# Where a fused kernel adds its weight sums: GpSimd, VectorE, and the buffers around them

## The chip, the cores and the metric

One core of one Trainium2 chip runs the whole program. The metric is the device time of one execution in microseconds (us), as a median of several executions. TensorE is the matrix engine, VectorE, ScalarE and GpSimd are the three elementwise engines; in the profile they are PE, DVE, ACT and POOL, and PEld is TensorE's loading of weights. PSUM is the memory into which TensorE writes; a bank is one of the kernel's tiles there, of 128 x 512 fp32, and its pools hold eight at a time (4 and 4 in the first chunk, then 3 for attention, 2 A, 1 B and 2 o). SBUF is the memory of the other tiles.

## The reference, cut to what matters

```python
B, H, S, D = 4, 8, 768, 48            # attention: a gated linear recurrence, fp32
f = 1 / (1 + exp(-f_logit))
for t in range(S):
    state = f[:, :, t, :, None] * state + einsum('bhd,bhe->bhde', k[:, :, t], v[:, :, t])
    y[:, :, t] = einsum('bhd,bhde->bhe', q[:, :, t], state)
x = y.transpose(0, 2, 1, 3).reshape(3072, 384)
out = (silu(x @ w_gate) * (x @ w_val)) @ w_out      # 384 -> 1536 -> 384, fp32
```

## The kernel before

The kernel works in six chunks of 128 positions for each of the four batches, so 512 tokens a chunk. While the feed-forward part of chunk c is written, attention of chunk c+1 is woven between its steps. A scheduler that knows the dependences orders each engine's instructions at build time; what the program writes first is not always what runs first.

The first chunk uses plain products. While they run, the weights still arrive and are joined from pieces by VectorE (four operations a piece: L455, L457, L458, L459). From the second chunk on, the two up projections are made by a scheme with 15 products of thirds instead of 18, and the down projection by one with 7 products of halves instead of 8. These need sums of weight blocks: 16 adds for the even 128-blocks, 16 for the odd ones, 4 for the down weights.

```python
# (cut) one group of 15 products, a "triple": (PSUM bank, weight block, token block)
PRODUCTS = [("A", "a11", "t14"), ("B", "a23", "t8"), ("o", "a21", "b22"),
            ("A", "a12", "t2"), ("B", "e3", "b32"), ("o", "e0", "t1"),
            ("A", "e5", "t9"), ("B", "e2", "t5"), ("c", "a13", "b11"),
            ("A", "e4", "t4"), ("B", "a33", "t15"), ("c", "a31", "t10"),
            ("A", "a32", "t11"), ("B", "e1", "t3"), ("A", "a22", "b21")]
...
def aside(name):                       # ScalarE copies the bank to SBUF, and so frees it
    return copy(name, "aside", bufs=3)
def finish(i, n, src):
    nc.scalar.activation(dst, src[:, 0, :], AF.Silu)              # L858 before, L848 after
    nc.vector.tensor_tensor(dst, dst, src[:, 1, :], ALU.mult)
...
                    elif r == 12:
                        minus(got[31], got[31], aside("A"))
                        finish(2, 0, got[31])
                    elif r == 13:
                        plus(got[11], got[11], p["B"])            # VectorE reads bank B itself
                        finish(0, 0, got[11])
                    else:
                        finish(1, 0, p["A"])
...
for c in range(NCH):
    if c == 0:
        hidden, last = mlp_plain(c)
        ...                                                       # the joins are put between steps
        pieces = hidden + [lambda: weight_sums(0, nc.gpsimd)] + last
    else:
        hidden, last = mlp_fifteen(c)
        pieces = hidden + last
    take_turns(pieces, attention_steps(c + 1) if c + 1 < NCH else [], 2 if c else 8)
    if c == 0:
        early.close()                                             # the first chunk's pools end here
        comb = ctx.enter_context(tc.tile_pool(name="comb", bufs=1))
        banks.append(ctx.enter_context(tc.tile_pool(name="bps", bufs=3, space=bass.MemoryType.PSUM)))
        banks_a, banks_b, banks_o = (
            ctx.enter_context(tc.tile_pool(name=f"{n}ps", bufs=k, space=bass.MemoryType.PSUM))
            for n, k in (("A", 2), ("B", 1), ("o", 2)))
        make_rooms(comb)
        load(SQUARES * B)
        down_weight_sums()
        weight_sums(1, nc.vector)
```

Lines to know: L666 are the first chunk's up projections, L690 its output products, L695 the copies of its outputs. L844 is the product of a triple (L834 after the change), L849 ScalarE's copy (L839), L933 and L987 the down products (L923 and L977). L728 and L731 are VectorE's add and subtract, wherever they are called from.

## Time and profile before

| | before |
|---|---|
| time, median of three runs | 674.54 us (673.98 to 674.97) |
| profiled span | 670.9 us |
| TensorE, VectorE, ScalarE, GpSimd busy | 628.1, 507.5, 273.9, 48.3 us |

The profiled execution took 672.67 us.

The lines that carry the argument are shown in the prediction. How the span divides: Four marks on TensorE cut it: the first up projection (L666), the first product of a triple (L844), and of the last down product (L987), which every chunk from the second on has, its first group in the program and its last but one.

| stretch of the kernel before | from, to (us) | long |
|---|---|---|
| opening | 0, 37.90 | 37.90 |
| first chunk | 37.90, 169.39 | 131.49 |
| second chunk | 169.39, 271.91 | 102.52 |
| third to sixth chunk | 271.91, 660.36 | 388.45 |
| closing | 660.36, 670.9 | 10.5 |

The opening is the same code in every kernel here, and it takes 36.3 to 38.1 us whatever the kernel; so below the first chunk is measured from its own start.

### The profile page before, as it was taken

The numbers are of one execution on the slowest core, as the hardware profiler recorded it, in microseconds if no ns is written. First come the engines' busy times: TensorE is split into PE (matmuls) and PEld (weight loads), VectorE is DVE, ScalarE is ACT, GpSimd is POOL, SyncE is SP. The second block draws the span as 40 slices with busy tenths as digits, with TensorE's granted clock in tenths as the row PEclk, the third lists the DMA queues.
The fourth block names the chain that finished last, engine by engine and source line by source line (L and its number), as shares of the span: only waits on it lengthen the run. The fifth ranks groups of instructions, "written<-read, shape, count | busy, mean of one in ns | idle before, by whom it ended". The sixth has DMA issues, their size and how long they took to land.

```text
span 670.9 us, 10581 instructions
## 1 busy us (share of the span) xinstructions
PE 628.1 (94%) x3894; PEld 503.5 (75%) x3894; DVE 507.5 (76%) x905; ACT 273.9 (41%) x504; POOL 48.3 (7%) x58
## 2 busy tenths in 40 slices
PE   7999999399999799999899999899999899999996
PEld 4955554165788689887689987679987689988895
DVE  5889689989789697579797679778769974457741
ACT  1466454110675352373471164461165440156500
POOL 1000008700000020000010000000000000000000
PEclk9999999599999799999999999999999989999999
DMA  9997543103323223402223401313302200100001
GB/s 176 212 222 215 139 152 110 59 4 110 111 56 81 55 60 88 113 25 74 69 59 86 117 24 48 95 48 91 104 19 57 65 22 13 60 2 1 0 1 52
DMA packets 98397, 51.92 MB, mean 77 GB/s; under 512 B 56864, under 2 KB 92192, under 8 KB 98336
## 3 DMA queue, kind: packets, MB, share of 16 engines
q1 hardware_dynamic: 95024, 46.63, 29.3%
q10 hardware_dynamic: 3312, 4.52, 1.9%
q8 instruction: 33, 0.54, 0.3%
q14 instruction: 28, 0.23, 0.1%
HBM read 42.47 MB, written 4.72 MB: 70 GB/s over the span
## 4 chain that ended last, share of the span: by engine, by line
PE 50%; DVE 20%; issue 5%; SPq 4%; ACT 4%; DMA 3%; POOL 0%; ACTq 0%; DVEq 0%; POOLq 0%
PE o L933 13%; PE A L844 11%; PE B L844 9%; PE o L844 4%; SPq L593 3%; DVE c L731 3%; PE c L844 3%; PE o L690 2%; PE sc L552 2%; PE o L987 2%; PE y L582 1%; DVE qT L532 1%; DMA xT<-yT 1%; DVE c L728 1%; DVE A L554 1%
## 5 line engine op out<-in xcount | busy, mean ns | idle before, releaser
L844 PE MATMUL A<-xs,w_both 128*128 128x256 f32 x240 | 65.5, 395 | 3.7 <-ACT ob L695 2.1
L933 PE MATMUL o<-w_out,h 128*128 128x192 f32 x360 | 62.5, 330 | 0.0
L933 PEld LDWEIGHTS o<-w_out,h 128*128 128x128 f32 x360 | 58.2, 190 | 1.8 <-ACT c L950 0.6
L844 PE MATMUL B<-xs,w_both 128*128 128x256 f32 x160 | 43.9, 397 | 14.4 <-DVE c L728 14.4
L858 ACT ACTIVATE h<-c 128x256 f32<-128x256 f32 x100 | 40.5, 416 | 40.1 <-DVE c L731 38.0
L844 PEld LDWEIGHTS A<-xs,w_both 128*128 128x128 f32 x240 | 46.1, 197 | 11.8 <-ACT ob L695 2.7
L849 ACT COPY c<-A 128x512 f32<-128x512 f32 x40 | 23.3, 583 | 74.8 <-PE A L844 41.0
L544 POOL TENSOR_TENSOR decayed<-state,tails 128x192 f32<-128x192 f32 x20 | 19.0, 950 | 476.8 <-DVE state L610 349.3
L849 ACT COPY aside<-A 128x512 f32<-128x512 f32 x60 | 35.1, 586 | 44.4 <-PE A L844 44.4
L728 DVE TENSOR_TENSOR c<-c,aside 128x512 f32<-128x512 f32 x40 | 28.1, 702 | 31.5 <-ACT aside L849 31.5
L731 DVE TENSOR_TENSOR c<-c,aside 128x512 f32<-128x512 f32 x60 | 41.7, 695 | 7.3 <-ACT aside L849 7.0
L690 PE MATMUL o<-w_out,h 128*128 128x384 f32 x96 | 35.0, 519 | 13.0 <-DVE h L682 13.0
L859 DVE TENSOR_TENSOR h<-h,c 128x256 f32<-128x256 f32 x100 | 41.1, 422 | 6.5 <-ACT h L858 6.5
L844 PEld LDWEIGHTS B<-xs,w_both 128*128 128x128 f32 x160 | 29.3, 193 | 20.9 <-DVE c L728 16.6
L844 PE MATMUL B<-xT,extra 128*128 128x256 f32 x160 | 42.3, 388 | 0.0
L731 DVE TENSOR_TENSOR c<-o,c 128x512 f32<-128x512 f32 x40 | 27.8, 694 | 18.8 <-PE o L844 17.4
L844 PE MATMUL c<-xT,w_both 128*128 128x256 f32 x160 | 41.2, 380 | 0.0
L844 PE MATMUL A<-xs,extra 128*128 128x256 f32 x160 | 41.2, 380 | 0.0
L933 PE MATMUL o<-ws,h 128*128 128x192 f32 x240 | 40.9, 326 | 0.0
L933 PEld LDWEIGHTS o<-ws,h 128*128 128x128 f32 x240 | 39.1, 190 | 0.1
L690 PEld LDWEIGHTS o<-w_out,h 128*128 128x128 f32 x96 | 18.7, 201 | 27.2 <-DVE h L682 14.8
L519 DVE TENSOR_TENSOR_SCAN tails<-gates,ones 128x516 f32<-128x516 f32 x24 | 30.5, 1270 | 8.9 <-POOL decayed L544 6.7
(140 smaller groups left out, 1245.8 us busy)
## 6 DMA issues: line engine op xcount, KB each, us to landing
fsquares<-in_f_logit_dram SPq DMA_DIRECT2D x64, 96.0 KB, 2.3
ksquares<-in_k_dram SPq DMA_DIRECT2D x64, 96.0 KB, 2.3
qsquares<-in_q_dram SPq DMA_DIRECT2D x64, 96.0 KB, 2.3
v<-in_v_dram SPq DMA_DIRECT2D x24, 192.0 KB, 3.6
w<-in_moe_w_gate_dram SPq DMA_DIRECT2D x6, 768.0 KB, 4.6
w<-in_moe_w_val_dram SPq DMA_DIRECT2D x6, 768.0 KB, 5.0
w<-in_moe_w_out_dram SPq DMA_DIRECT2D x6, 768.0 KB, 4.5
out_dram<-ob ACTq DMA_DIRECT2D x23, 192.0 KB, 2.1
```

The source lines that it names most:

```text
L519: nc.vector.tensor_tensor_scan(tail[:, 0:n][:, ::-1], gate[:, 0:n][:, ::-1], ones[:, ::-1], 1.0, op0=ALU.mult, op1=ALU.add)
L544: nc.gpsimd.tensor_tensor(decayed[:, :, 0:D], states[b], whole.broadcast_to((128, HP, D)), ALU.mult)
L552: nc.tensor.matmul(sc[par][:, a * C:(a + 1) * C], lhsT=kT[r, a, :], rhs=qT[r, a, :], start=True, stop=True)
L593: nc.sync.dma_start(out=xT[c][f % 128:f % 128 + n, f // 128, b * C:(b + 1) * C], in_=yT[r:r + n, par, a // 2 * C:(a // 2 + 1) * C])
L690: nc.tensor.matmul(p, lhsT=h[n // 2][:, n % 2 * 2 + b // 2, b % 2 * C:(b % 2 + 1) * C], rhs=w_out[:, j, :], start=(n == 0), stop=(n == NF ...
L728: (engine or nc.vector).tensor_tensor(dst, a, b, ALU.add)
L731: (engine or nc.vector).tensor_tensor(dst, a, b, ALU.subtract)
L844: nc.tensor.matmul(p[name][:, n, :], lhsT=weights_of[a][:, n, cols], rhs=tokens[b], start=fresh and n == 0, stop=True, skip_group_check=True)
L849: nc.scalar.copy(t, p[name])
L858: nc.scalar.activation(dst, src[:, 0, :], AF.Silu)
L859: nc.vector.tensor_tensor(dst, dst, src[:, 1, :], ALU.mult)
L933: nc.tensor.matmul(p[:, n, :], lhsT=lhsTs[j][:, n * C:(n + 1) * C], rhs=rhs[:, j, :], start=first and j == 0 and n == 0, stop=j == NP - 1, ...
```

## The change

The intent: GpSimd's sums slow VectorE (a 128x512 sum took 1.75 us beside them and 0.68 without), so VectorE makes them all, placed where they are needed and no sooner; bank B, the only single one, is freed by ScalarE and not by the busy VectorE; and the banks A, B and o are laid where they come free earlier.

```diff
-            pieces = hidden + [lambda: weight_sums(0, nc.gpsimd)] + last
+            pieces = hidden + weave(last, weight_sums(0))           # in pairs, by VectorE
         else:
             hidden, last = mlp_fifteen(c)
+            if c == 1:
+                half = len(hidden) // 2
+                hidden = hidden[:1] + weave(hidden[1:half], weight_sums(1)) + hidden[half:]
+                hidden.append(lambda: behind(down_weight_sums))
...
-            banks.append(ctx.enter_context(tc.tile_pool(name="bps", bufs=3, ...)))
-            banks_a, banks_b, banks_o = (... for n, k in (("A", 2), ("B", 1), ("o", 2)))
+            banks_a, banks_b, banks_o, later = (... for n, k in (("A", 2), ("B", 1), ("o", 2), ("b", 3)))
+            banks.append(later)
             make_rooms(comb)
             load(SQUARES * B)
-            down_weight_sums()
-            weight_sums(1, nc.vector)
...
-                        plus(got[11], got[11], p["B"])
+                        plus(got[11], got[11], aside("B"))
...
+    def behind(f):                     # edges: what f writes on VectorE runs after what was written before
+        n = len(traced)
+        last = next(ins for ins in reversed(traced) if ins.engine == mybir.EngineType.DVE)
+        f()
+        keep_order([last] + [ins for ins in traced[n:] if ins.engine == mybir.EngineType.DVE])
```

More of the change, by code (lines that the diff above doesn't have):

```diff
@@ L725, in short_path, with plus, minus @@
     sums = {}
-    def plus(dst, a, b, engine=None):
-        (engine or nc.vector).tensor_tensor(dst, a, b, ALU.add)
-    def minus(dst, a, b, engine=None):
-        (engine or nc.vector).tensor_tensor(dst, a, b, ALU.subtract)
+    def plus(dst, a, b):
+        nc.vector.tensor_tensor(dst, a, b, ALU.add)
+    def minus(dst, a, b):
+        nc.vector.tensor_tensor(dst, a, b, ALU.subtract)
     def minus_both(dst, a, b):
@@ L745, in weight_parts, with weight_sums @@
         return w, e
-    def weight_sums(odd, engine):
+    def weight_sums(odd):
         w, e = weight_parts()
@@ L751, in weight_sums @@
         a11, a12, a13, a21, a22, a23, a31, a32, a33 = (w[i, k] for i in range(3) for k in range(3))
-        add, sub = (lambda d, x, y: plus(d, x, y, engine)), (lambda d, x, y: minus(d, x, y, engine))
-        sub(e[0], a11, a12)
-        add(e[1], a12, a33)
-        add(e[1], e[1], a13)
-        sub(e[2], e[1], a11)
-        sub(e[3], e[0], a13)
-        add(e[4], a21, a32)
-        sub(e[5], a12, a21)
-        sub(a11, a12, a23)
-        add(a13, e[3], a21)
-        add(e[3], e[3], a23)
-        add(a13, a13, a31)
-        sub(a13, a13, a33)
-        sub(a21, a22, a21)
-        add(a22, a22, a23)
-        add(a22, a22, a32)
-        sub(a31, a32, a31)
+        return [lambda f=f, d=d, x=x, y=y: f(d, x, y) for f, d, x, y in (
+            (minus, e[0], a11, a12), (plus, e[1], a12, a33), (plus, e[1], e[1], a13), (minus, e[2], e[1], a11),
+            (minus, e[3], e[0], a13), (plus, e[4], a21, a32), (minus, e[5], a12, a21),
+            (minus, a11, a12, a23), (plus, a13, e[3], a21), (plus, e[3], e[3], a23), (plus, a13, a13, a31),
+            (minus, a13, a13, a33), (minus, a21, a22, a21), (plus, a22, a22, a23), (plus, a22, a22, a32),
+            (minus, a31, a32, a31))]
     down_sums = {}
@@ L993, in down_seven, with weave @@
         return hidden_sums, [one, two, three, four]
+    def weave(first, second):
+        second = [second[i:i + 2] for i in range(0, len(second), 2)]
+        woven = []
+        for i, f in enumerate(first):
+            woven += [f] + [lambda fs=fs: behind(lambda: [g() for g in fs]) for fs in
+                            second[i * len(second) // len(first):(i + 1) * len(second) // len(first)]]
+        return woven
+    def behind(f):
[3 more added lines that the diff above has]
+        keep_order([last] + [ins for ins in traced[n:] if ins.engine == mybir.EngineType.DVE])
     def take_turns(first, second, rest):
@@ L1073, in short_path @@
             comb = ctx.enter_context(tc.tile_pool(name="comb", bufs=1))
-            banks.append(ctx.enter_context(tc.tile_pool(name="bps", bufs=3, space=bass.MemoryType.PSUM)))
-            banks_a, banks_b, banks_o = (
+            banks_a, banks_b, banks_o, later = (
                 ctx.enter_context(tc.tile_pool(name=f"{n}ps", bufs=k, space=bass.MemoryType.PSUM))
-                for n, k in (("A", 2), ("B", 1), ("o", 2)))
+                for n, k in (("A", 2), ("B", 1), ("o", 2), ("b", 3)))
+            banks.append(later)
             make_rooms(comb)
             load(SQUARES * B)
-            down_weight_sums()
-            weight_sums(1, nc.vector)
         if c == NCH - 2:
```

## The prediction

> **What bounds the kernel now.** I read the page's busy shares first, then its forty slices, then the lists of waits, then TensorE and VectorE in order of time around the slices where TensorE is not full.
>
> ```profile
> PE 628.1 (94%) x3894; PEld 503.5 (75%) x3894; DVE 507.5 (76%) x905; ACT 273.9 (41%) x504; POOL 48.3 (7%) x58
> PE   7999999399999799999899999899999899999996
> POOL 1000008700000020000010000000000000000000
> PEclk9999999599999799999999999999999989999999
> ```
>
> TensorE is the bound nearly everywhere. Its hole, in slice eight (117 to 134 us), lies where GpSimd is busy, and the granted clock drops there too. TensorE's own timeline, start and duration first, the wait in brackets:
>
> ```profile
> 114.52 1.56 PE L690 MATMUL o<-w_out,h 128*128 128x384 f32 x4
> 123.40 1.65 PE L690 MATMUL o<-w_out,h 128*128 128x384 f32 x2 [7.33 <-DVE h L682]
> 130.76 5.16 PE L690 MATMUL o<-w_out,h 128*128 128x384 f32 x10 [5.71 <-DVE h L682]
> 149.00 18.33 PE L690 MATMUL o<-w_out,h 128*128 128x384 f32 x56
> 169.39 1.13 PE L844 MATMUL A<-xs,w_both 128*128 128x256 f32 x4 [2.06 <-ACT ob L695]
> 223.56 2.07 PE L844 MATMUL B<-xs,w_both 128*128 128x256 f32 x4 [3.80 <-DVE c L728]
> 330.32 1.13 PE L844 MATMUL B<-xs,w_both 128*128 128x256 f32 x4 [3.03 <-DVE c L728]
> ```
>
> The first chunk's output products (L690) stop 7.3 and 5.7 us: two of their four PSUM banks hold the last two up projections until VectorE has multiplied them into h. The next chunk's first product then waits 2.06 us for the last output copy. Later stops are on bank B, whose last sum VectorE reads. Why is h late? VectorE in order of time, the same operations with GpSimd running (first three) and after it (last three):
>
> ```profile
> 116.00 1.61 DVE L457 TENSOR_SCALAR top<-top 128x768 int32<-128x768 int32 x1
> 117.54 1.75 DVE L731 TENSOR_TENSOR extra<-extra,w_both 128x512 f32<-128x512 f32 x1
> 119.21 2.01 DVE L458 SCALAR_TENSOR_TENSOR top<-w,top 128x768 int32<-128x768 int32 x1
> 133.58 0.80 DVE L457 TENSOR_SCALAR top<-top 128x768 int32<-128x768 int32 x1
> 134.31 0.68 DVE L728 TENSOR_TENSOR extra<-w_both 128x512 f32<-128x512 f32 x1
> 134.91 0.94 DVE L458 SCALAR_TENSOR_TENSOR top<-w,top 128x768 int32<-128x768 int32 x1
> ```
>
> Each SBUF operation costs about one microsecond more while GpSimd's sixteen sums run (102.4 to 129.0 us). VectorE also does odd-block weight sums ahead of the h products: the scheduler had hoisted work written later. The waits' totals (sum, count, longest):
>
> ```profile
> PE B L844 <- DVE c L728: 14.4, 7, 3.8
> ACT h L858 <- DVE c L731: 38.0, 33, 3.2
> ```
>
> The first line: seven stops of TensorE on bank B. The second: ScalarE too is held by VectorE.
>
> [...] Here the 3.80 us stop was followed by products of about 1.7 us instead of 0.86, the 3.03 us stop by none.
>
> **The change part by part.**
>
> *GpSimd's sums go.* From 102.7 to 130.1 us VectorE ran, at slow durations, three L457 (4.86 us), two L455 (3.25), two L458 (4.03), two L459 (3.47), five adds (8.78) and a scan (2.28). At undisturbed durations (0.56, 0.56, 0.96, 0.95, 0.68, 1.22) they take 1.68, 1.12, 1.92, 1.90, 3.40 and 1.22. The excess is 26.67 - 11.24 = 15.4 us. The five odd-block adds (3.4 us undisturbed) are also put behind later work. So the two h products, done at 123.3 and 130.7, should follow their matmuls, the last of which ends near 112.5.
>
> *What TensorE then needs.* Unstopped from 112.44: 96 output matmuls at 0.327 (18.33/56) are 31.4 us; attention between them (2.1 + 0.9 + 1.6 + 2.6) 7.2. That ends at 151.0, and the next chunk's first product now starts at 169.4: at most 18.4 us, of which 13.0 are the stops, 2.9 slow clock behind them (1.65 - 0.65 and 5.16 - 3.27), 2.06 plus a few tenths the boundary. The PSUM rearrangement is aimed at the last: A, B and o come onto banks that attention held, and not the output products.
>
> *VectorE in that stretch.* Four joins of 3.03 us (12.1), attention 6.3, two h 1.4, sixteen even-block sums at 0.68 now moved here (10.9), eleven token sums (4.1): 34.8 of 38.6 us. It fits, tightly. With the weave, by the step arithmetic, the last attention step comes after output step six and not after step four, so five steps (13.1 us) follow it and not seven. Its copy, transfer and token sums took 148.3 to 161.0, or 12.7 us. So the first product will be at 151 to 157; I choose 154.4, a gain of 15.
>
> *The second chunk pays.* It ran from 169.4 to 273.9. Up to 243.8 VectorE was busy 12.75 + 14.28 + 14.95 + 17.04 = 59 of 74.4 us (windows). The odd-block sums add 16 x 0.68 = 10.9 to its first half; about 8 us of the next attention, done at 161 to 170 ahead of the boundary, move behind it. That is 78 us of VectorE against 67 of TensorE (74.4 less the 3.80 stop and 3.2 of slow clock): VectorE becomes its bound, say 81 with little idle time. The four down-weight sums (1.34 to 1.36 each, 5.4 us) go to the output stage, where VectorE is busy 24.2 of 30.2: perhaps 1 us. That is +7 us from this view. Counting only VectorE's whole work from 112 to 274 (137.6 less about 10 of contention plus 12 net sums, 140, against 162 elapsed) with 8 us idle leaves the two chunks together 14 shorter, not 8. I take 11.
>
> *Bank B.* Twenty copies on ScalarE (0.586 each, 11.7 us in all, at 41% busy) replace a wait for VectorE; the adds stay at 0.68 to 0.70. The stops in chunks three to five are 1.01 + 3.03 + 0.67 + 3.04 + 0.42 + 2.48 = 10.7 us. ScalarE sits behind VectorE itself in its SiLU, and the next triple's third A product needs a ScalarE copy in that same queue, so a stop of 3 us can give about two products, 1.7 us: 5.1 + 1 of the small ones, 6 us of 10.7.
>
> Sum: -11 - 6 = -17 us gives 657.5; I put 1.5 us of it aside for order effects of a static schedule: 659.0 us.
>
> **The rivals.** *VectorE takes over entirely.* For it: the 78 against 67 us[...]. Against: today's own stop at 223.6 came from such a burst and cost only 7. It would eat the gain: 666 to 672. *The stops go whole.* For it: the h products have nothing left to wait for, chunk two's half-clock stretch may vanish, ScalarE has room for B. Then 18 + 10, less 3: near 649. *The boundary is hidden by transfers:* if the last attention step, written later, makes the xT transfers (issue to 154.98, landing at 156.4) end no sooner relative to the output products, the token sums set the start and the gain falls to 10: about 664.
>
> **Range and chances.** The sizes that I am least sure of are the second chunk (+0 to +12) and B (0 to -11); the 15 us rest on stops seen in the trace. So 648 to 668 for 8 in 10. Two per cent of 674.54 is 13.5, so "faster" means under 661.0: my value lies 2 us on that side, chance 0.57; within 2% 0.41; slower 0.02.
>
> **What would show it.** GpSimd busy near 19 + 3 us without sums; no VectorE L457 or L458 over 1.2 us; the L690 stops gone and the clock full in slice eight; the first "A" product at 151 to 157 without a wait on the output copy; sixteen 128x512 adds among the second chunk's first two triples, VectorE over 90% busy there, and new TensorE stops; that chunk longer than 104.5 us; the waits of B on L728 gone, A or B waiting on ScalarE instead. I am wrong if the two long stops stay in another form (a join, a transfer), or if the second chunk loses over 12 us.

## The result, and the profile after

| | before | after |
|---|---|---|
| time, median of four runs each | 674.75 us (673.98 to 676.73) | 643.21 us (642.67 to 644.62) |
| ratio | | 0.9531 (0.9506 to 0.9557) |
| profiled span | 670.9 us | 641.5 us |
| first chunk | 131.49 | 112.52 |
| second chunk | 102.52 | 100.46 |
| third to sixth chunk | 388.45 | 381.96 |
| opening and closing | 48.4 | 46.6 |

A ratio here and below is the mean time of one kernel's fast runs over the mean of the other's fast runs of the same rounds, so it is not quite the ratio of the medians that stand beside it. The kernel after ran in two more batches, at 0.9576 and 0.9583; the mean of its three ratios, 0.956, is what its variants are held against.

The gain is twice the predicted one: 31.5 us by the medians, against 15.5. The time lies below the range of 648 to 668. By the two profiles the gain is 29.4 us, because the profiled execution of the kernel before was a short one.

The page of the kernel after, first the busy times, then the forty slices of TensorE, GpSimd and TensorE's granted clock:

```profile
PE 615.1 (96%) x3894; PEld 495.8 (77%) x3894; DVE 498.4 (78%) x921; ACT 286.6 (45%) x526; POOL 29.9 (5%) x42
PE   7999999999998999999899999899999999999996
POOL 1000000000000050000020000020000000000000
PEclk8999999999999999999999999999999999999999
```

The hole in TensorE's eighth slice is gone, and so are all slices with a lowered clock after the first; before there were three of them. TensorE's busy time itself fell by 13 us with the same 3894 matmuls: a busy time is shorter at full clock (four products of bank B behind a stop took 1.13 us at full clock, at 306.43 in the kernel after, and 2.07 at half clock, at 223.56 in the kernel before). Windows of the three stretches split each into TensorE's busy time and the rest of its length, its idle time:

| stretch | before: busy + idle | after: busy + idle | less busy | less idle |
|---|---|---|---|---|
| first chunk | 116.24 + 15.25 | 112.52 + 0.00 | 3.72 | 15.25 |
| second chunk | 98.12 + 4.40 | 94.69 + 5.77 | 3.43 | -1.37 |
| third to sixth | 375.24 + 13.21 | 371.53 + 10.43 | 3.71 | 2.78 |

Of the 27.5 us that the three stretches lost, 16.7 are stops and 10.9 are shorter busy time. Most of the latter is slow clock: in these stretches TensorE was busy for 18.0 us at half clock in the kernel before and not at all in the kernel after, and half of that is 9.0. In what follows, "lost at half clock" is this half, an estimate from the trace.

TensorE in order of time at the end of the first chunk:

```profile
110.72 2.75 PE L690 MATMUL o<-w_out,h 128*128 128x384 f32 x8
113.74 5.33 PE L690 MATMUL o<-w_out,h 128*128 128x384 f32 x16
...
136.21 13.17 PE L690 MATMUL o<-w_out,h 128*128 128x384 f32 x40
149.22 1.03 PE L834 MATMUL A<-xs,w_both 128*128 128x256 f32 x4
```

No bracket, so no wait: the output products run through, and the first product of a triple follows them without a stop. The VectorE lines of that stretch answer to those of the prediction; the last of these four is its longest idle time there:

```profile
110.39 0.56 DVE L457 TENSOR_SCALAR top<-top 128x768 int32<-128x768 int32 x1
110.87 0.68 DVE L682 TENSOR_TENSOR h<-h,val 128x512 f32<-128x512 f32 x1
111.47 0.95 DVE L458 SCALAR_TENSOR_TENSOR top<-w,top 128x768 int32<-128x768 int32 x1
...
136.40 0.35 DVE L610 TENSOR_TENSOR state<-decayed,dS 128x192 f32<-128x192 f32 x1 [2.93 <-PE dS L606]
```

The join operations are back at 0.56 and 0.95 us, where they had taken 1.61 and 2.01 beside GpSimd, and the last product of h is written at 111.5 and not at 130.7 us. VectorE even waits for TensorE.

Windows give the busy time of each engine in a stretch. The second chunk up to its down products, of the kernel before:

```profile
core 0: us, PE busy (x) PEld busy (x) DVE busy (x) ACT busy (x) POOL busy (x), PEclk, DMA share, GB/s
169.39:243.80 74.41, 70.01 (x445) 57.06 (x445) 59.02 (x106) 44.85 (x84) 1.34 (x2) 0.95 0.28 74
```

The end of the first chunk and the same part of the second, of the kernel after:

```profile
110.72:149.22 38.50, 38.50 (x227) 24.27 (x226) 29.63 (x53) 9.04 (x15) 1.07 (x4) 1.00 0.20 51
149.22:220.78 71.56, 66.51 (x445) 54.53 (x444) 70.46 (x127) 46.83 (x87) 1.86 (x3) 1.00 0.34 88
```

VectorE is busy 70.46 of 71.56 us, 98%. Yet this part is shorter than it was before, when VectorE was busy 59.02 of 74.41. TensorE's stops in it, beside waits of under half a microsecond, are two:

```profile
179.11 1.16 PE L552 MATMUL sc<-qT,kT 48*128 48x128 f32 x16 [1.38 <-DVE qT L540]
199.90 1.16 PE L552 MATMUL sc<-qT,kT 48*128 48x128 f32 x16 [1.97 <-DVE qT L540]
```

In the third to sixth chunk bank B no longer waits for VectorE, but it still waits, for ScalarE's copy (TensorE's timeline of the kernel after):

```profile
306.43 1.13 PE L834 MATMUL B<-xs,w_both 128*128 128x256 f32 x4 [2.46 <-ACT aside L839]
...
407.85 1.13 PE L834 MATMUL B<-xs,w_both 128*128 128x256 f32 x4 [1.62 <-ACT aside L839]
```

ScalarE's own order of time shows why: its copy of B stands behind a SiLU that waits for VectorE.

```profile
305.48 0.42 ACT L848 ACTIVATE h<-c 128x256 f32<-128x256 f32 x1 [3.57 <-DVE c L731]
305.81 0.57 ACT L839 COPY aside<-B 128x512 f32<-128x512 f32 x1
```

### The profile page after: what moved, and what is told of

It is laid out like the page before. It is cut to its first block, busy times and chain, and to the rows that moved or that the text cites.

```text
span 641.5 us, 10613 instructions
## 1 busy us (share of the span) xinstructions
PE 615.1 (96%) x3894; PEld 495.8 (77%) x3894; DVE 498.4 (78%) x921; ACT 286.6 (45%) x526; POOL 29.9 (5%) x42
## 4 chain that ended last, share of the span: by engine, by line
PE 60%; DVE 19%; SPq 7%; DMA 5%; ACT 3%; issue 3%; POOL 0%; DVEq 0%; ACTq 0%; POOLq 0%
PE o L923 13%; PE A L834 9%; PE B L834 8%; SPq L593 5%; PE gate L666 5%; PE val L666 5%; PE sc L552 3%; PE o L834 3%; PE o L690 3%; DVE c L731 3%; PE c L834 2%; PE o L977 2%; PE y L582 2%; DMA ksquares<-in_k_dram 2%; DVE tails L519 1%
## 5 line engine op out<-in xcount | busy, mean ns | idle before, releaser
L834 PE MATMUL A<-xs,w_both 128*128 128x256 f32 x240 | 63.1, 383 | 3.6 <-ACT c L839 2.4
L728 DVE TENSOR_TENSOR c<-c,aside 128x512 f32<-128x512 f32 x60 | 41.9, 698 | 26.8 <-ACT aside L839 26.7
L923 PEld LDWEIGHTS o<-w_out,h 128*128 128x128 f32 x360 | 58.1, 190 | 2.8 <-DVE w_out L731 0.6
L848 ACT ACTIVATE h<-c 128x256 f32<-128x256 f32 x100 | 40.4, 416 | 34.8 <-DVE c L731 30.9
L834 PEld LDWEIGHTS A<-xs,w_both 128*128 128x128 f32 x240 | 44.2, 190 | 11.6 <-ACT c L839 4.1
L544 POOL TENSOR_TENSOR decayed<-state,tails 128x192 f32<-128x192 f32 x20 | 27.0, 1351 | 480.4 <-DVE state L610 331.7
L834 PE MATMUL B<-xs,w_both 128*128 128x256 f32 x160 | 42.6, 388 | 6.2 <-ACT aside L839 5.7
L731 DVE TENSOR_TENSOR c<-c,aside 128x512 f32<-128x512 f32 x60 | 41.7, 696 | 5.8 <-ACT aside L839 5.6
L839 ACT COPY aside<-B 128x512 f32<-128x512 f32 x60 | 35.0, 583 | 13.1 <-PE B L834 13.1
L731 DVE TENSOR_TENSOR c<-o,c 128x512 f32<-128x512 f32 x40 | 27.8, 696 | 10.6 <-PE o L834 8.8
L552 PEld LDWEIGHTS sc<-qT,kT 48*128 48x128 f32 x384 | 25.0, 187 | 14.0 <-issue 10.0
```

What stands on the lines that cost most here:

```text
L544: nc.gpsimd.tensor_tensor(decayed[:, :, 0:D], states[b], whole.broadcast_to((128, HP, D)), ALU.mult)
L552: nc.tensor.matmul(sc[par][:, a * C:(a + 1) * C], lhsT=kT[r, a, :], rhs=qT[r, a, :], start=True, stop=True)
L728: nc.vector.tensor_tensor(dst, a, b, ALU.add)
L731: nc.vector.tensor_tensor(dst, a, b, ALU.subtract)
L834: nc.tensor.matmul(p[name][:, n, :], lhsT=weights_of[a][:, n, cols], rhs=tokens[b], start=fresh and n == 0, stop=True, skip_group_check=True)
L839: nc.scalar.copy(t, p[name])
```

## The experiments

The theory is the prediction's: GpSimd's contention with VectorE made the first chunk's hole, bank B made the later stops, and each part of the change acts where it seems to. The rivals: the gain comes from moving and holding the sums, whoever makes them; or from the PSUM pools, which the prediction gave two microseconds; or the second chunk is better for a reason of its own. The experiments ran in four batches on three chips (the first and the last batch on the same one), each beside the kernel before (medians 673.21, 673.40, 673.17 and 672.37).

The marks, in us, from the profiled execution of each kernel:

| kernel | median | ratio to before | first chunk | second | third to sixth |
|---|---|---|---|---|---|
| before | 674.75 | 1 | 131.49 | 102.52 | 388.45 |
| after | 643.21 | 0.9531 | 112.52 | 100.46 | 381.96 |
| e6_after_again | 646.13 | 0.9576 | 112.51 | 101.65 | 383.12 |
| e14_after_third | 645.42 | 0.9583 | 112.51 | 102.15 | 381.28 |
| e1_gpsimd_back | 654.86 | 0.9720 | 123.25 | 101.89 | 381.48 |
| e2_vector_only | 663.50 | 0.9859 | 120.54 | 102.24 | 388.24 |
| e3_pools_back | 649.22 | 0.9640 | 115.73 | 102.58 | 382.06 |
| e4_b_back | 653.89 | 0.9708 | 112.51 | 100.17 | 393.04 |
| e5_no_edges | 643.37 | 0.9548 | 114.42 | 98.21 | 382.29 |
| e7_fewer_odd (wrong numbers) | 642.29 | 0.9527 | 112.51 | 98.34 | 383.18 |
| e8_half_early | 643.42 | 0.9548 | 112.51 | 99.48 | 382.87 |
| e9_copy_first | 646.92 | 0.9605 | 112.51 | 101.02 | 384.35 |
| e10_both | 646.89 | 0.9604 | 112.51 | 100.88 | 384.42 |
| e11_b_only | 661.69 | 0.9820 | 132.11 | 100.23 | 380.86 |
| e12_pools_only | 664.87 | 0.9878 | 129.67 | 95.95 | 389.35 |
| e13_three_parts | 645.08 | 0.9588 | 119.40 | 98.03 | 380.65 |

### e1: the even sums back on GpSimd

```diff
-            pieces = hidden + weave(last, weight_sums(0))
+            pieces = hidden + [lambda: [f() for f in weight_sums(0, nc.gpsimd)]] + last
```

(The functions of the sums take an engine again.)

> The changed kernel with one part undone: the sixteen even-block sums run on GpSimd again, after the last up projection, as before; the odd-block sums stay in the second chunk. Contention theory[...]: joins and adds between 100 and 130 us last 1.6 to 2.0 us again, about 10 to 15 us of excess, the first product of the second chunk starts at 155 to 163 us instead of 149.2, the whole takes 650 to 657 us. Order theory (the gain came from holding the odd-block sums back): h is multiplied in time all the same, first product by 152, whole within 3 us of 643.2.

Measured: 654.86 us, 0.972 (0.9689 to 0.975) of before, so 1.6% of 673, 11 us, over the kernel after. The first chunk is 10.7 us longer and nothing else is. TensorE's timeline has the stop again, and VectorE's has the slow joins, one fence for each:

```profile
120.98 1.65 PE L690 MATMUL o<-w_out,h 128*128 128x384 f32 x2 [6.06 <-DVE h L682]
```

```profile
114.84 1.61 DVE L457 TENSOR_SCALAR top<-top 128x768 int32<-128x768 int32 x1
118.31 2.02 DVE L458 SCALAR_TENSOR_TENSOR top<-w,top 128x768 int32<-128x768 int32 x1
```

The durations are those of the kernel before to within 0.01 us, with everything else of the change in place. The edit also takes the weaving of these sums away; e2 changes their engine alone. Together they show that the engine of these sums is what stretches VectorE's work and stops TensorE.

### e2: the even sums by VectorE, and nothing else

```diff
-            pieces = hidden + [lambda: weight_sums(0, nc.gpsimd)] + last
+            pieces = hidden + [lambda: weight_sums(0, nc.vector)] + last
```

> The kernel before with one part done: the sixteen even-block sums on VectorE, nothing held, nothing else changed. Contention theory: no instruction of VectorE over 1.4 us there, the first product at 151 to 158 instead of 169.4, whole 656 to 663 us. Order theory: some 28 sums of 0.6 us (17 us) stand ahead of the last two h products, so TensorE's stops on L690 stay at 8 us or more, first product after 162, whole 667 to 673 us.

Measured: 663.50 us, 0.9859 (0.9829 to 0.9889): 9.5 us of gain, all in the first chunk (10.95 us shorter). It does not reach the kernel after's first chunk, because a shorter stop stands in place of the two:

```profile
120.52 7.12 PE L690 MATMUL o<-w_out,h 128*128 128x384 f32 x16 [3.41 <-DVE w_out L459]
...
157.30 1.13 PE L844 MATMUL A<-xs,w_both 128*128 128x256 f32 x4 [2.09 <-ACT ob L695]
```

TensorE now waits for a join and not for h: the sixteen even sums stand on VectorE between 101.6 and 116.6 us, ahead of that join's operations. The time is half a microsecond above the expected 656 to 663. The 16 products after the stop take 7.12 us where they take 5.33 at full clock. The 2.09 us at the boundary stay, and the second chunk's 3.80 us stop on B stays too.

### e3: the old PSUM pools in the new kernel

```diff
-            banks_a, banks_b, banks_o, later = (... for n, k in (("A", 2), ("B", 1), ("o", 2), ("b", 3)))
-            banks.append(later)
+            banks.append(ctx.enter_context(tc.tile_pool(name="bps", bufs=3, ...)))
+            banks_a, banks_b, banks_o = (... for n, k in (("A", 2), ("B", 1), ("o", 2)))
```

> The changed kernel with the PSUM pools in the old order. If the banks mattered: the first A product of the second chunk waits again for the last output copy, 2 to 4 us later than 149.2, and the whole takes 645 to 648 us. If the token sums set that start anyway: within 1 us of 643.2.

Measured: 649.22 us, 0.964 (0.9611 to 0.9669), 0.8% or 5 us over the kernel after. The first chunk is 3.2 us longer, by this wait:

```profile
153.63 1.16 PE L834 MATMUL A<-xs,w_both 128*128 128x256 f32 x4 [3.06 <-ACT ob L695]
```

The second chunk is 0.4 to 2.1 us longer than in the three looks at the kernel after; a stop of 2.92 us with lowered clock behind it has appeared in it. This difference is clock alone: the chunk lost 3.4 us at half clock here, and 0 to 1.7 in the three looks. Both expectations were too low: the pools are worth more than the boundary's two microseconds.

### e4: bank B read by VectorE again

```diff
-                        plus(got[11], got[11], aside("B"))
+                        plus(got[11], got[11], p["B"])
```

> The changed kernel with bank B's last sum read from PSUM by VectorE again. If the copy by ScalarE was worth what the prediction gave it: stops of TensorE on L728 come back, 10 us or so in chunks three to five, whole 648 to 651 us; since VectorE is busy 98% in the second chunk of the changed kernel, B may be held longer there than before, up to 655. Rival (ScalarE stands behind VectorE anyway, so the copy only moves the wait): within 2 us of 643.2.

Measured: 653.89 us, 0.9708 (0.967 to 0.9746), 1.5% or 10 us over the kernel after. The second chunk loses nothing, against the second half of the expectation, the third to sixth 11.1 us:

```profile
308.44 2.07 PE L834 MATMUL B<-xs,w_both 128*128 128x256 f32 x4 [4.24 <-DVE c L728]
...
413.75 2.07 PE L834 MATMUL B<-xs,w_both 128*128 128x256 f32 x4 [3.04 <-DVE c L728]
```

Read the second number: four such products take 1.13 us at full clock behind a stop, and 2.07 here. Of the 11.1 us, 7.5 are TensorE's busy time (379.02 against 371.53) and 3.6 its idle time. The kernel before has a stop of 3.04 us too, and in its profile it looks harmless:

```profile
433.30 1.13 PE L844 MATMUL B<-xs,w_both 128*128 128x256 f32 x4 [3.04 <-DVE c L728]
434.27 1.65 PE L844 MATMUL o<-xT,w_both 128*128 128x256 f32 x4
435.71 1.91 PE L844 MATMUL A<-xs,w_both 128*128 128x256 f32 x4
```

It is not: the first four products run at full speed, and the clock falls 1.2 us after the stop's end. So the price of a stop differs, from nothing (3.03 us at 330.32 in the kernel before) over half clock for 3.4 us to half clock for 6.8 us (e4's, at half clock from 412.62 to 419.45), and it may come after the group that one looks at.

What decides between these can be read from the traces. In each trace all changes of the granted clock after its first record lie on one grid of 3.413 us, to within 2 ns. Lay the grid over TensorE's records of all 16 profiles, from the first up projection to the last mark. Of the cells at full clock, all 27 in which TensorE was idle for over 0.58 of the cell were followed by a cell at half clock, 6 of the 12 with 0.49 to 0.58 were, and none of the 2720 with less. At half clock, full clock came back after each of the 33 cells with an idle share up to 0.13, and after none of the 19 with 0.14 or more. So two stops of one length can be dear and free by where they fall on the grid (3.04 and 3.03 us here). Two pairs of cells of the kernel before show it (TensorE's busy time is the second number, the clock the third from the end); the end of a cell cuts the stop before 330.32 into 1.43 and 1.60 us, and the one before 433.30 into 0.86 and 2.18:

```profile
325.31:328.72 3.41, 1.99 (x10) 1.33 (x8) 3.31 (x8) 0.69 (x2) 0.00 (x0) 1.00 0.10 22
328.72:332.14 3.42, 1.82 (x8) 1.63 (x9) 2.63 (x7) 1.79 (x4) 0.00 (x0) 1.00 0.43 111
431.12:434.53 3.41, 1.23 (x6) 1.10 (x7) 3.21 (x7) 1.21 (x4) 0.00 (x0) 1.00 0.65 157
434.53:437.94 3.41, 3.41 (x10) 2.67 (x9) 0.69 (x1) 0.86 (x2) 0.00 (x0) 0.50 0.35 83
```

By stops, in the same 16 profiles: no stop of 1.01 to 1.66 us was followed by a lowered clock, 6 of 12 from 1.68 to 2.28 us were, 15 of 22 from 2.42 to 3.06, and all 15 from 3.19 up (three of these began at half clock). The fall came up to 1.6 us after the stop's end (e6).

The kernel does not place the grid: in the three profiles of the kernel after (after, e6, e14) the stop near 200 us ended 3.4, 1.8 and 2.4 us after a cell's start. A single profile's stretch can therefore be some 1.7 us longer or shorter for each such stop by chance (half of a cell of 3.413 us; e6 and e14 lost 1.7 each, the kernel after nothing).

### e5: no edges

```diff
         f()
-        keep_order([last] + [ins for ins in traced[n:] if ins.engine == mybir.EngineType.DVE])
```

> The changed kernel without the ordering edges: the sums are written where the change writes them, but the scheduler may hoist them. In its order all thirty-two sums and three of the four down-weight sums now stand ahead of the second chunk's token sums. If the edges are what spares the first chunk: 0.6 us for each of the sixteen odd sums and about 4 us for the others go on VectorE between 110 and 149 us, where it has 8.9 us idle; the first product slips by 4 to 8 us and the second chunk, with VectorE relieved, is 3 to 5 us shorter than 100.5: whole 643 to 648 us. If holding mattered a lot, as the name of the change suggests: over 650. If it did nothing: 642 to 644.

Measured: 643.37 us, 0.9548 (0.9509 to 0.9587), the same as the kernel after (0.956). The first chunk is 1.9 us longer, with one stop of 1.20 us for a join, and the second 2.3 to 3.9 us shorter (1.7 to 2.3 without what two of the three looks lost at half clock). The edges move work across the boundary and buy nothing in the whole that these runs can tell.

### e6 and e14: the kernel after again

No edit: the same kernel in other batches, beside its variants.

> The changed kernel itself, for comparison on the same chip: 643 us, ratio 0.953 to the kernel before.

> The changed kernel again, on the same chip as the three parts: 643 to 646 us.

Measured: 646.13 us, 0.9576 (0.9533 to 0.9619), and 645.42 us, 0.9583 (0.9551 to 0.9614). Over its three batches the kernel's medians spread by 2.9 us. The profiled execution of e6 shows one source, the clock. The same stop, 2.46 us in the kernel after, was followed there by a full clock for all of the next 10 us; here by this:

```profile
308.78 2.07 PE L834 MATMUL B<-xs,w_both 128*128 128x256 f32 x4 [2.42 <-ACT aside L839]
310.64 1.63 PE L834 MATMUL o<-xT,w_both 128*128 128x256 f32 x4
```

In the second chunk, the stop of 1.97 us had no slow clock behind it in the kernel after; the same stop of 1.99 us in e6 and of 2.00 us in e14 had, and these chunks lost 1.7 us each at half clock. Without it the three chunks are 99.9 to 100.5 us long.

### e7: nine of the odd sums left out

Wrong numbers (relative error 2.9), to take 5.4 us of VectorE's work out of the second chunk.

```diff
-                hidden = hidden[:1] + weave(hidden[1:half], weight_sums(1)) + hidden[half:]
+                hidden = hidden[:1] + weave(hidden[1:half], weight_sums(1)[:7] + [lambda: None] * 9) + hidden[half:]
```

> Wrong numbers on purpose: nine of the sixteen odd-block sums left out, the rest where the change has them. What does the second chunk pay for them? The prediction had VectorE become that chunk's bound and pay microsecond for microsecond: 5.4 us of sums less would then shorten the chunk by 5. If TensorE's stops there (1.38 and 1.97 us before the score products and a few of 0.2 to 0.5) are all that it pays: 2 to 4 us shorter, whole 639 to 641. If the load isn't what stops TensorE: within 1 us.

Measured: 642.29 us, 0.9527 (0.9487 to 0.9567); the second chunk 98.34 us, 2.1 to 3.8 shorter than in the three looks at the kernel after. Two of these three had lost 1.7 us at half clock, and e7's chunk none: without it the gain is 1.6 to 2.1. Were VectorE the bound there outright, 5.4 us less of its work would have made it 5.4 shorter. About a third came through. The whole time, above the expected 639 to 641, is not clearly different.

### e8: half of the odd sums in the first chunk's end

```diff
-            pieces = hidden + weave(last, weight_sums(0))
+            pieces = hidden + weave(last, weight_sums(0) + weight_sums(1)[:8])
...
-                hidden = hidden[:1] + weave(hidden[1:half], weight_sums(1)) + hidden[half:]
+                hidden = hidden[:1] + weave(hidden[1:half], weight_sums(1)[8:]) + hidden[half:]
```

(The bundles are kept at eight in both places.)

> A try at something better: eight of the sixteen odd sums (4.8 us) woven into the end of the first chunk, where VectorE of the changed kernel has 8.9 us idle of 38.5, the other eight left in the second. If the idle time there can be used: first product within 1 us of 149.2 and the second chunk 2 to 3 us shorter, whole 640 to 642 us. If the token sums get pushed back behind the sums: first product at 151 to 154 and no gain, 643 to 646.

Measured: 643.42 us (643.26 to 643.58), 0.9548 (0.951 to 0.9586). The first chunk is not a hundredth longer: VectorE had the room. The second is 1.0 to 2.7 us shorter, 0.5 to 1.0 without the half clock. Against the kernel after's 0.956 the total is within the interval.

### e9: the copy of B ahead of the SiLUs

ScalarE's copy of B stood behind a SiLU that waits for VectorE. Here the last two SiLUs are written after the copy, and ScalarE is held to that order.

```diff
                         minus(got[32], got[32], p["c"])
-                        finish(2, 1, got[32])
                     elif r == 12:
                         minus(got[31], got[31], aside("A"))
-                        finish(2, 0, got[31])
                     elif r == 13:
-                        plus(got[11], got[11], aside("B"))
+                        spare = aside("B")
+                        n0 = len(traced) - 1
+                        plus(got[11], got[11], spare)
+                        finish(2, 1, got[32])
+                        finish(2, 0, got[31])
                         finish(0, 0, got[11])
+                        keep_order([ins for ins in traced[n0:] if ins.engine == mybir.EngineType.Activation])
```

> A try at something better, and a test of why the copy of bank B doesn't end all stops there: in the changed kernel ScalarE copies B only after a SiLU that waits for VectorE (stops of 2.46, 1.62 and 1.38 us in chunks three to five). Here the two SiLUs of output block three are traced after that copy and held behind it. If ScalarE's order is what holds B: those stops go and the whole takes 638 to 641 us. If the stop only moves on to the next A product, which waits for another ScalarE copy behind the same SiLUs: 642 to 645.

Measured: 646.92 us, 0.9605 (0.9564 to 0.9645), no gain, and above both expectations. The waits of B went, and a longer one came on A, whose copy into the next triple's first sum now stands behind the same SiLUs:

```profile
309.73 1.54 PE L834 MATMUL A<-xs,w_both 128*128 128x256 f32 x4 [3.47 <-ACT c L839]
...
412.88 2.08 PE L834 MATMUL A<-xs,w_both 128*128 128x256 f32 x4 [2.65 <-ACT c L839]
```

In both kernels VectorE works almost only on attention from about 300.5 to 304 us and again from about 306 to 307, while ScalarE's SiLUs wait for its sums. I read the stop as belonging to this burst, and the bank that shows it as a matter of order; that is argued from one other order only.

### e10: e8 and e9 together

```diff
# the edits of e8 and of e9, both
```

> The same with half of the odd sums woven into the end of the first chunk (which by itself gave 643.4 and a second chunk 1 us shorter). If the two add up: 637 to 640 us; if neither pays: 642 to 645.

Measured: 646.89 us, 0.9604 (0.9566 to 0.9642), the same as e9. This settles only that there is nothing in it.

### e11: only the copy of B

```diff
-                        plus(got[11], got[11], p["B"])
+                        plus(got[11], got[11], aside("B"))
```

(In the kernel before.)

> The kernel before with one part done: ScalarE copies bank B's last sum. The stops on L728 (14.4 us) go; some of 1.4 to 2.5 us on the ScalarE copy take their place; the second chunk loses its 3.80 us stop with the slow clock behind it. By the size in the prediction (6 us of 10.7 in chunks three to five, nothing counted in the second): 667 us. By what undoing it cost in the changed kernel (10.7 us): 663 us.

Measured: 661.69 us, 0.982 (0.9783 to 0.9856): 12.1 us of gain. In the profiled execution the second chunk is 2.3 and the third to sixth 7.6 us shorter. No stop after the second chunk's first product is over 1.7 us, and in the third to sixth chunk the granted clock is 1.00 in the mean, where it was 0.99. By the prediction's term it would have been 6; it is twice that.

### e12: only the PSUM pools

The edit of e3 the other way round, in the kernel before.

```diff
-            banks.append(ctx.enter_context(tc.tile_pool(name="bps", bufs=3, ...)))
-            banks_a, banks_b, banks_o = (... for n, k in (("A", 2), ("B", 1), ("o", 2)))
+            banks_a, banks_b, banks_o, later = (... for n, k in (("A", 2), ("B", 1), ("o", 2), ("b", 3)))
+            banks.append(later)
```

> The kernel before with one part done: the PSUM pools in the new order. If the wait for the last output copy is all that they take away there: 2 to 4 us less, 669 to 671.5 us. If the first products of the next chunk have to wait for their token sums or weight sums anyway: 673.

Measured: 664.87 us, 0.9878 (0.9841 to 0.9916): 8.2 us of gain. The boundary gave 1.8 us, about what the prediction had for it. The second chunk gave 6.6, which was in no theory, so both expectations were missed. Windows of the whole second chunk, of the kernel before and then of e12:

```profile
169.39:271.91 102.52, 98.12 (x656) 83.97 (x657) 81.45 (x152) 49.23 (x91) 5.71 (x4) 0.97 0.28 72
```

```profile
166.42:262.37 95.95, 93.67 (x657) 81.41 (x656) 83.63 (x156) 50.50 (x93) 2.47 (x4) 1.00 0.30 79
```

TensorE's idle time fell from 4.4 to 2.3 us (the length less PE busy), and its busy time by 4.5, most of it by the clock, whose mean rose from 0.97 to 1.00 (3 us of 102). The 3.80 us stop on B with 2.07 us products behind it has become this one:

```profile
218.22 1.13 PE L844 MATMUL B<-xs,w_both 128*128 128x256 f32 x4 [2.28 <-DVE c L728]
```

That no slow clock follows this stop is in part chance: the end of a cell of the grid, at 217.30 us, cuts it. The order of products in that chunk differs from the kernel before's: with other pools the scheduler placed attention's pieces elsewhere. Which of its moves did it was not tested.

### e13: the three parts, with nothing woven, moved or held

```diff
-            pieces = hidden + [lambda: weight_sums(0, nc.gpsimd)] + last
+            pieces = hidden + [lambda: weight_sums(0, nc.vector)] + last
# and the edits of e11 and e12; the odd and down sums stay where the kernel before has them
```

> The kernel before with three parts of the change done at once, each of which was run alone (even sums by VectorE: 9.5 us; bank B by ScalarE: 12.1; pools: 8.2), and without the rest: no sums moved into the second chunk, none woven, none held. If the parts add up and moving and holding only shift work about: 673 less 29.8, so 642 to 646 us. If moving the odd sums and weaving the even ones are a part of the gain of their own: 647 to 652. If the parts overlap (less slow clock to save for each): 649 to 655.

Measured: 645.08 us (643.3 to 649.05, six runs), 0.9588 (0.9553 to 0.9622), beside 0.9583 for the kernel after in the same batch. The three parts make the whole gain, as far as the intervals can tell. Its first chunk is 6.9 us longer than the kernel after's, again with a stop for a join at lowered clock, and its later chunks make up for it within what the runs can tell:

```profile
121.77 8.29 PE L690 MATMUL o<-w_out,h 128*128 128x384 f32 x16 [3.37 <-DVE w_out L459]
```

## Why the prediction was right or wrong

By the marks of the two profiles, against the prediction's own sum:

| term | predicted | measured |
|---|---|---|
| first chunk, with the boundary | -15 | 112.52 - 131.49 = -19.0 |
| second chunk | +4 (the "11 for both" less 15) | 100.46 - 102.52 = -2.1 |
| third to sixth chunk (bank B) | -6 | 381.96 - 388.45 = -6.5 |
| set aside for order effects | +1.5 | 0 |
| opening and closing | 0 | -1.2 and -0.7 |
| sum | -15.5 | -29.4, before rounding |

The largest miss is the second chunk (6.1 us), the next the margin on the first (4.0).

**Right: the cause of the hole.** Step one said that GpSimd's sums stretch VectorE by 15.4 us and so hold h. e1 brings the stop back, and e2, by the engine alone, takes it away. Undone it costs 10.7 us of trace, alone it gives 10.95. In the kernel before, beside GpSimd's adds of 1.26 to 2.00 us, VectorE's operations were some 1.05 us longer each, whatever their own length: 0.56 to 1.61 (L457), 0.68 to 1.75 (L731), 0.96 to 2.01 (L458). By what means GpSimd does this, no run shows. Its working came close too: "at most 18.4" against 19.0, with 15.25 of stops where 13.0 and 2.06 stood, and 3.72 of busy time where 2.9 of slow clock stood. One of its lines is misread: the L457 of 0.80 us, called "after" GpSimd, ran beside a small operation of GpSimd (132.66 to 133.97); undisturbed it takes the 0.56 us of the sum.

**Right, but sized with a margin that was not needed: the first chunk.** Unstopped TensorE was worked out to end at 151.0; measured from the kernel before's opening, the first product is at 37.90 + 112.52 = 150.4. The step that failed is the choice of 154.4 in place of that figure, which allowed for VectorE (34.8 of 38.6 us) and the last token sums setting the start. VectorE was busy 29.63 of 38.50: by the operations of the window, the joins took 8.1 us there and not 12.1, since the rest were done before it, and one h product lay in it, not two. The last token sum ended 2 us ahead of the first product. Seven further profiles (e4, e6 to e10, e14) have 112.51, the length without stops.

**Wrong: "The second chunk pays".** This is the term with the largest error, 6.1 us. It has two halves. That VectorE would be over 90% busy came true (98%), and TensorE did get new stops, but of 1.38 and 1.97 us. The step that failed is from "78 us of VectorE against 67 of TensorE" to "say 81": VectorE's work there was 70.46 us and not 78, and the part took 71.56. The sizes were nearly right as single durations: by the trace's records these sum to 67.4 us in that part before and to 84.4 after, 17 more where 18.9 were added. But instructions that follow each other closely overlap (two 128x512 sums took 1.28 us after the change, and not twice 0.68), so the busy time rose by 11.4 only. Moving the odd sums there does cost something: against e13, which leaves them in the first chunk, the second chunk is 2.4 to 4.1 us longer in the three looks (3.6 to 4.1 without the half clock), and TensorE's idle time in it rose by 1.37 us over the kernel before. The other half is what the prediction did not put into its sum: the chunk's old loss, the 3.80 us stop and its slow clock, went, and with the clock 3.43 us of busy time. e12 shows that the pools alone can take it away with no sum moved, e11 that B's copy alone takes 2.3 us; with all three parts (e13) the chunk is 4.5 us shorter. These do not add up, because each edit gives another order; in the new kernel, undoing the pools costs this chunk only 0.4 to 2.1 us, all of it clock, and undoing B's copy nothing.

**Wrong in size: the PSUM pools.** "2.06 plus a few tenths" was right at the boundary (1.8 us alone, 3.2 undone). The whole is 8.2 us alone and about 5 undone. The failed assumption is that pools act only where a bank is handed over.

**Bank B: right in one profile by luck, for a wrong reason, and too small in the times.** The predicted 6 us stand against 6.5 in these two profiles, and the predicted form came true: waits on ScalarE, behind its SiLU. But the 6 us were to be idle time, and TensorE's idle time fell by 2.78 only; 3.71 us are shorter busy time, 3.4 of them by the clock. The step that failed is the one that priced the stops: "the 3.03 us stop by none" is true of that stop, at 330.32, but behind the 3.04 us stop at 433.30 and the 2.48 us one at 535.49 the same profile has half clock for some 3.4 us each, beginning over a microsecond after the stop's end. At half speed that is 1.7 us of loss each, which the sum of 10.7 us left out. Executions differ besides, since the grid of e4 falls differently on them: the copy alone gives 12.1 us (e11) and undone costs 10 (e4). Seven runs of the kernel before, beside e5 to e8, lie between a span of 669.6 us at a mean clock of 0.979 and one of 675.4 at 0.965; the profile that the prediction read (670.9) is one of the shorter ones. Over all profiles, the third to sixth chunk is 388.2 to 393.0 us long where VectorE reads B (before, e2, e4, e12; mean 389.8) and 380.7 to 384.4 where ScalarE copies it (the others; mean 382.4): 7.4 us.

**The rivals.** "The stops go whole ... near 649" named the mechanism that came true in the first two chunks. "VectorE takes over entirely" came true as far as VectorE's share (98%), but did not eat the gain: its work was less than counted, and the new stops brought no slow clock here and 1.7 us of loss in e6 and e14. The half clock does not need a stop as long as the 3.80 us of the kernel before: 1.99 us was enough (e6). "Hidden by transfers" fell with the token sums done 2 us early. The rival that the stated intent suggests, that placing and holding the sums makes the gain, fell with e5 and e13.

**By parts.** Alone, in time: the sums' engine 9.5, the copy of B 12.1, the pools 8.2, in sum 29.8 us. The three together (e13) gave 27.7 (0.0412 x 673), the kernel after 28 to 31.5. The profile's signs read as foretold in most points: no L457 or L458 over 1.2 us, the L690 stops gone with the clock full in slice eight, B waiting on ScalarE. Three missed: GpSimd busy 29.9 us and not 22, the first product at 149.2 and not in 151 to 157, and the second chunk shorter than 104.5 us. GpSimd's excess is one operation:

```profile
224.35 8.73 POOL L544 TENSOR_TENSOR decayed<-state,tails 128x192 f32<-128x192 f32 x1 [28.78 <-DVE state L610]
```

It takes 0.52 us in the median. Here it lies beside a run of VectorE's adds and subtracts in SBUF without a pause (224.12 to 233.36), the down sums among them, and ends at 233.08. I read this as the same contention in the other direction; no run tests it apart.

**Open.** Which move of the schedule in the second chunk makes e12's 6.6 us; and what decides the clock behind a cell that is idle for 0.49 to 0.58 of its length. No variant beats the kernel after by more than its intervals: e5 and e13 are equal to it and simpler, e8 is equal, e7 computes something else.

## What to carry to other kernels

An idle engine is not free help: compare the durations of the busy one's instructions with and without it (1.61 and 0.56 us for L457 here). Count a stop of the matrix engine of some 1.7 us or more with the slow clock that may follow it (in these profiles it followed none of the stops of 1.01 to 1.66 us and 6 of 12 from 1.68 to 2.28), look for that clock in the microseconds behind the stop and not only in the first group, and take several executions before one profile's clock becomes the rule. Try the parts of a change alone: a line about buffers can be worth more than the placement on which most of the code was spent, since it changes the order of everything after it.
